# Attention and gated feed-forward on one core: a second queue for the first loads, sign words on a choice of engine, two scales from a sum

## The chip, the core and the metric

The kernel runs on one NeuronCore of a Trainium2 chip. The core has a matrix engine (TensorE, PE in the profile), a vector engine (VectorE, DVE), a scalar engine (ScalarE, ACT), a general engine (GpSimd, POOL) and an engine that issues most transfers (SyncE, SP). Each engine works through its own list of instructions in order, and semaphores tie the lists together. The metric is the device time of one execution in microseconds, lower is better.

## What is computed

Causal attention over 4 batches of 12 heads with 448 tokens of 64 values, then a two-layer feed-forward with a sigmoid gate over the 1792 tokens (768 to 2048 to 768 values):

```python
scores = scale * np.matmul(q, k.transpose(0, 1, 3, 2))
scores = np.where(np.triu(np.ones((seq, seq), dtype=bool), k=1), -1000000000.0, scores)
attn = np.exp(scores - np.max(scores, axis=-1, keepdims=True))
attn = attn / (np.sum(attn, axis=-1, keepdims=True) + 1e-09)
attn_out = np.matmul(attn, v)
x = attn_out.transpose(0, 2, 1, 3).reshape(B * S, H * D)
h = x @ w_in
g = h * (1.0 / (1.0 + np.exp(-1.702 * h)))
out = g @ w_out
```

q, k and v are float32. The weights are float64 and arrive as pairs of 32-bit words.

## The kernel before

**Precision.** Most matmuls take numbers as two float16 parts (a rounded part and the rest), so that a product is three float16 matmuls. The scale that puts the numbers into float16's range is a power of two, found from sums of squares or from the diagonal of a product with itself. `gram` (L609) makes this product on TensorE, `gram_max` (L625) takes the largest value of each row on VectorE, `all_max` (L414) spreads the values of all partitions over a row by a matmul with an identity (`one16`) and takes the largest again, and `norm_scale` (L433) makes the power of two with integer operations on one column. This is done for each slice of w_in ("wi"), for w_out ("wo"), for v, and for each pair of units of k ("k", from a sum of squares on ScalarE).

**Weights.** `to_f32` (L551) makes float32 out of the word pairs in four passes: a scale-down by ScalarE or VectorE (L555), the low words (L563, either engine), the sign words (L586, VectorE) and a combining pass on VectorE (L597). `w_in_slice` (L632) does this for 8 slices of 256 columns. A slice is loaded in two halves of 768 KB into a part of `wob`, all on SP. The slices 0 to 2 (`TUNE["early"]`) are converted in halves of 768 columns, the other ones in one go of 1536. Then `split` (L479) writes the two float16 parts into `wib`. `w_out_load` and `w_out_split` do the same for 16 pieces of w_out; these are parked in unused parts of `wob` and `vraw`.

**Attention.** A batch has 6 units of two heads, and the tokens of a batch form two blocks of 4 and 3 chunks of 64. In batch 0 all units work in float32: `k_unit32` (L900) and `q_unit32` (L917) load heads, turn them on TensorE against `ident` (L885, into `ps_t`, a part of `ps_o`) and copy them into `kT` and `qT`. `q_unit32` writes the two heads of a unit into separate quarters of a `qT` that POOL has filled with zeros, so that one contraction over 128 rows gives one head in each half of the columns (`scores32`, L1081, by `halves`, L409). `chunk` (L1105) adds the mask and finds the row maximum on VectorE (L1112) and exponentiates on ScalarE (L1126); the probabilities are divided, turned on TensorE (L883) into `PT`, and multiplied by v (L1268). From batch 1 on the same is done in float16 parts with transposing transfers.

**Feed-forward.** Each block's tokens go through `h_slice` (L1327): 72 matmuls into a bank of `ps_h`, a tanh on ScalarE (L1362), the gate multiply on VectorE (L1367), and the split into `gT`. The first block alternates between two banks. `out_tile` (L1380) multiplies by w_out (L1405).

**Order.** The kernel's functions don't issue instructions; they add operations with estimated costs to a list (`Ops.add`). `Ops.order` (L103) makes the list of each engine by a search over priorities with random tries that start from `SEED`, and for operations that two engines can do it picks the engine too. So a changed cost or a changed operation can move instructions everywhere.

## Time and profile before

| | us |
|---|---|
| median of 3 runs | 605.53 |
| lowest and highest | 603.63, 605.74 |
| the profiled execution | 605.29 |
| its span, first to last instruction | 603.54 |
| TensorE busy | 575.1 |
| VectorE busy | 416.6 |
| ScalarE busy | 351.6 |
| GpSimd busy | 59.2 |

The page gives the busy time of each engine, its course in 40 slices of about 15 us, the chain of work that ended last, and the costliest groups of instructions. A group names a line, an engine, an operation, what it writes and reads, how often, the busy time, the mean of one instruction, and the idle time of the engine before it. The trace behind the page can be asked for stretches of time (windows), for instructions in order of time, and for groups that keep shapes apart. Matmuls overlap, so that the mean of one is longer than its share of the busy time; float32 matmuls stand as two records each.

### The profile page before, as it was taken

What the parts mean: (1) busy time and instruction counts of PE and PEld (TensorE: products, weight loads), DVE (VectorE), ACT (ScalarE), POOL (GpSimd) and SP (SyncE); (2) the same over time, 40 slices, a digit from 0 to 9 for tenths busy, and PEclk for the clock granted to TensorE, in tenths of its full rate; (3) what the DMA queues carried; (4) which work ended last, traced back from release to release, by engine and by line L of the source; (5) the groups of instructions that cost most, each with busy time, mean ns of one, the idle gap of its engine ahead of it and who ended that gap; (6) DMA issues with size and microseconds to landing.
All of it is one profiled execution on the core that took longest, in us unless ns stands there. A gap on an engine that the chain in (4) does not pass through costs nothing.

```text
span 603.5 us, 22259 instructions
## 1 busy us (share of the span) xinstructions
PE 575.1 (95%) x9526; PEld 501.7 (83%) x9526; DVE 416.6 (69%) x1164; ACT 351.6 (58%) x835; POOL 59.2 (10%) x162
## 2 busy tenths in 40 slices
PE   3876999999999999999999999999999999999997
PEld 2555867886699799977888899998999999889986
DVE  2999999999996889977489887978777122203100
ACT  4888899887866767754676465666355122203110
POOL 3000000012120121212111210211100000000000
PEclk9989899999999999999999999999999999999999
DMA  8998478554498987899997899575835400000000
GB/s 270 277 288 281 128 251 302 173 127 110 86 177 156 142 163 112 167 176 153 156 158 115 155 161 174 105 128 120 130 59 68 94 2 15 1 28 3 28 28 27
DMA packets 201604, 79.90 MB, mean 132 GB/s; under 512 B 182304, under 2 KB 191264, under 8 KB 201504
## 3 DMA queue, kind: packets, MB, share of 16 engines
q1 hardware_dynamic: 201504, 78.47, 61.5%
q8 instruction: 74, 1.21, 0.9%
q14 instruction: 26, 0.21, 0.1%
HBM read 41.68 MB, written 5.51 MB: 78 GB/s over the span
## 4 chain that ended last, share of the span: by engine, by line
PE 68%; DVE 4%; ACT 2%; DMA 1%; issue 1%; SPq 0%; DVEq 0%; ACTq 0%
PE ps_o L1405 33%; PE ps_h L412 26%; PE ps_s L1089 4%; PE ps_v L1268 4%; DVE z L1112 1%; DMA vraw<-in_v_dram 1%; ACT p L472 1%; PE ps_s L412 1%; DVE p L477 1%; PE ps_h L883 1%; DVE ps_h L1367 0%; ACT waste L462 0%; DMA kf<-in_k_dram 0%; DVE q L477 0%; DVE gT L477 0%
## 5 line engine op out<-in xcount | busy, mean ns | idle before, releaser
L412 PE MATMUL ps_h<-xT,wib 128*64 128x256 f16 (+1 forms) x4608 | 244.4, 260 | 0.1
L1405 PE MATMUL ps_o<-wob,gT 128*64 128x384 f16 x2688 | 239.8, 326 | 0.8 <-DVE wob L477 0.6
L412 PEld LDWEIGHTS <-wib 128*64 128x64 f16 x4608 | 226.3, 110 | 7.9 <-issue 2.1
L1405 PEld LDWEIGHTS <-gT 128*64 128x64 f16 x2688 | 171.8, 110 | 38.3 <-issue 3.2
L1126 ACT ACTIVATE z<-z,cols 128x320 f32<-128x320 f32 (+6 forms) x168 | 84.1, 501 | 51.6 <-DVE cols L1112 49.1
L1367 DVE SCALAR_TENSOR_TENSOR ps_h<-t,ps_h 128x512 f32<-128x512 f32 (+1 forms) x64 | 40.1, 626 | 82.4 <-ACT t L1362 82.0
L1362 ACT ACTIVATE t<-ps_h,cols 128x512 f32<-128x512 f32 (+1 forms) x64 | 40.3, 629 | 72.1 <-PE ps_h L412 68.0
L1112 DVE CUSTOM_DVE_ANT_0 z<-ps_s,mask,cols 128x128 f32<-128x128 f32 (+6 forms) x126 | 57.2, 479 | 18.0 <-PE ps_s L1089 17.4
L477 DVE SCALAR_TENSOR_TENSOR p<-z,cols,p 128x128 f16<-128x128 f32 (+3 forms) x126 | 63.2, 528 | 1.5 <-ACT p L472 0.8
L477 DVE SCALAR_TENSOR_TENSOR gT<-ps_h,gT 128x512 f16<-128x512 f32 (+1 forms) x64 | 39.7, 620 | 13.5 <-ACT gT L472 13.1
L1268 PE MATMUL ps_v<-PT,v 128*64 128x192 f16 (+7 forms) x792 | 44.7, 257 | 0.5 <-DVE cols L453 0.4
L1089 PE MATMUL ps_s<-kT,qT 128*64 128x64 f16 (+4 forms) x504 | 41.5, 273 | 1.2 <-DVE cols L1112 0.9
L472 ACT ACTIVATE p<-z,cols 128x384 f16<-128x384 f32 (+3 forms) x66 | 34.0, 533 | 13.3 <-DVE cols L1235 9.7
L472 ACT ACTIVATE gT<-ps_h 128x512 f16<-128x512 f32 (+1 forms) x53 | 28.9, 545 | 20.4 <-DVE ps_h L1367 20.3
L472 ACT ACTIVATE ob<-ps_o,cols 128x384 f32<-128x384 f32 x24 | 13.8, 577 | 45.0 <-PE ps_o L1405 44.6
L1126 ACT ACTIVATION_READ_ACCUMULATOR z<-z,cols 128x1 f32 x168 | 31.6, 188 | 0.0
L412 PE MATMUL ps_s<-kT,qT 128*64 128x320 f32 (+6 forms) x168 | 25.0, 409 | 5.6 <-DVE cols L1112 5.6
L1268 PEld LDWEIGHTS <-v 128*64 128x64 f16 x648 | 29.2, 110 | 1.0
L1089 PEld LDWEIGHTS <-qT 128*64 128x64 f16 x504 | 24.7, 110 | 4.3 <-issue 1.3
L1047 POOL TENSOR_SCALAR q<-q 128x512 f16<-128x512 f16 (+1 forms) x32 | 21.9, 686 | 50.8 <-ACT q L472 26.6
L474 DVE TENSOR_SCALAR p<-z,cols 128x256 f16<-128x256 f32 (+3 forms) x60 | 24.6, 422 | 1.3
L472 ACT ACTIVATE wob<-wob 128x768 f32<-128x768 f32 (+1 forms) x20 | 21.8, 1091 | 5.5 <-DMA wob<-in_moe_w_in_dram 5.0
(98 smaller groups left out, 564.9 us busy)
## 6 DMA issues: line engine op xcount, KB each, us to landing
wob<-in_moe_w_in_dram SPq DMA_DIRECT2D x16, 768.0 KB, 6.5
wob<-in_moe_w_out_dram SPq DMA_DIRECT2D x9, 768.0 KB, 6.2
vraw<-in_moe_w_out_dram SPq DMA_DIRECT2D x7, 768.0 KB, 6.7
out_dram<-ob SPq DMA_DIRECT2D x28, 192.0 KB, 2.2
kf<-in_k_dram SPq DMA_DIRECT2D x36, 112.0 KB, 3.3
vraw<-in_v_dram SPq DMA_DIRECT2D x9, 384.0 KB, 5.0
qf<-in_q_dram SPq DMA_DIRECT2D x48, 64.0 KB, 3.1
qf<-in_q_dram SPq DMA_DIRECT2D x48, 48.0 KB, 3.2
```

What stands on the lines that cost most here:

```text
L412: nc.tensor.matmul(out[o : o + 64], lhsT[:, o : o + 64], rhs, start=start, stop=stop)
L472: nc.scalar.activation(out=dst, in_=src, func=AF.Copy, scale=sc)
L474: nc.vector.tensor_scalar(out=dst, in0=src, scalar1=sc, scalar2=None, op0=ALU.mult)
L477: nc.vector.scalar_tensor_tensor(out=dst, in0=src, scalar=sc, in1=hi, op0=ALU.mult, op1=ALU.subtract)
L1047: nc.gpsimd.tensor_scalar(out=dst, in0=src, scalar1=1.0, scalar2=1.0, op0=ALU.mult, op1=ALU.mult)
L1089: nc.tensor.matmul(ps[64 * j : 64 * j + 64], qt[:, g, i - c0, 64 * j : 64 * j + 64], kt[:, : i + 1, 64 * j : 64 * j + 64], start=(g == 0), ...
L1112: lambda e: nc.vector.tensor_tensor_reduce(out=z[:, :w], in0=ps, in1=mask[:, S - w :], scale=c, scalar=3.0e38, op0=ALU.add, op1=ALU.min, a ...
L1126: lambda e: nc.scalar.activation(out=z[:, :w], in_=z[:, :w], func=AF.Exp, bias=m, scale=-1.0, accum_out=l),
L1268: nc.tensor.matmul(ps[64 * j : 64 * j + 64, 64 * (first - c0) : w], vt[:, J, j] if f32(b, u) else vt[:, gv, J, j, :], (p_f32(pi)[:, at] if ...
L1362: lambda e: nc.scalar.activation(out=th, in_=ph, func=AF.Tanh, scale=ts[:, sl : sl + 1]),
L1367: lambda e: nc.vector.scalar_tensor_tensor(out=ph, in0=th, scalar=1.0, in1=ph, op0=ALU.add, op1=ALU.mult),
L1405: nc.tensor.matmul(po[64 * j : 64 * j + 64, :OH], gT[:, f, gg, 64 * r : 64 * r + 64], wo_pair(f, gw, nh), start=(f == 0 and gg + gw == 0), ...
```

## The change

It does these things:

- The four loads of the slices 0 and 1 of w_in (`beside=2`) are issued by ScalarE, on its own queue ("AQ" in the planner), ahead of everything else on that engine. All other loads stay on SP.
- All 8 slices are converted in halves (`early=8`).
- The sign words can be made by ScalarE as well: a copy to float16 of numbers that have been scaled down to almost nothing leaves only the sign.
- For k and w_out, `all_max` puts a matmul with a column of ones (`total`) in place of the spread and of the maximum; the sum over the partitions, one column, is read by `norm_scale` from PSUM.
- `q_unit32` copies both heads of a unit at once and needs no zeros; `scores32` contracts over 64 rows for each head.
- The planner knows the second queue, has a lower cost for issuing a load, and starts from another seed, so all lists are ordered anew.

```diff
@@ TUNE, Ops
-    early=3,
+    early=8,
+    beside=2,
-SEED = 2
+SEED = 1
-    ENGINES = ("SP", "PE", "ACT", "DVE", "POOL")
+    ENGINES = ("SP", "AQ", "PE", "ACT", "DVE", "POOL")
-    LOAD = 0.68
+    LOAD = 0.5
+    BESIDE = 1.4
...
@@ kernel
+    ones16 = cols[:, 174:175].bitcast(BF16)[:, 0:1].to_broadcast([P, 64])
+    def total(out, src):
+        for o in range(0, P, 64):
+            nc.tensor.matmul(out[o : o + 64], ones16, src, start=True, stop=True)
...
@@ all_max
+        if tag in ("k", "wo"):
+            half = src.bitcast(BF16)[:, 1:2]
+            add(
+                {"PE": 0.03},
+                lambda e: total(row[:, :1], half),
+                [src_key, "one16"], row_keys, prio,
+            )
+            return row[:, :1], row_keys[0]
...
@@ to_f32
+        def sign(e):
+            if e == "ACT":
+                nc.scalar.activation(
+                    out=words(dst, F16, 2)[..., 1], in_=words(raw, F32, 2)[..., 1], func=AF.Copy
+                )
+            else:
...
         add(
-            dve(n, rate=0.521),
...
+            {**dve(n, rate=0.521), **act(n, rate=1.0)},
+            sign,
             raw_keys, dst_keys, prio,
         )
@@ w_in_slice
-                {"SP": Ops.LOAD},
-                lambda e, h=h: nc.sync.dma_start(
+                {"AQ" if s < TUNE["beside"] else "SP": Ops.LOAD},
+                lambda e, h=h: (nc.scalar if e == "AQ" else nc.sync).dma_start(
@@ q_unit32
-        if stale[t]:
...
-        for j in range(2):
...
+        add(
+            {**act(64 * ni, psum=True, rate=1.2), **dve(64 * ni, rate=1.2)},
+            lambda e: scaled(e, qt.rearrange("p (x t) -> p x t", t=2), got, 1.0),
+            [got_key], [key], prio,
+        )
+        return qt, key, -QK_SCALE, None
@@ scores32
-                halves(ps, qt[:, i - c0].rearrange("p j w -> p (j w)"), kt[:, : 64 * (i + 1)], True, True)
+                for j in range(2):
+                    x = slice(64 * j, 64 * j + 64)
+                    nc.tensor.matmul(
+                        ps[x], qt[x, 64 * (i - c0) : 64 * (i - c0) + 64], kt[x, : 64 * (i + 1)], start=True, stop=True
+                    )
@@ the end
-        for i, e in ops.order():
+        for i, e in sorted(ops.order(), key=lambda x: x[1] != "AQ"):
```

SP's list, which issues the loads, at its start, before. `q_76` and `qf` are the buffers of the first k and q heads, `wob` takes the weight halves, `v_70` to `v_72` the first v:

```order
L875 DMA q_76<-in_k_dram 128x128 x2
L648 DMA wob<-in_moe_w_in_dram 128x3x512
L875 DMA qf<-in_q_dram 128x128 x2
L648 DMA wob<-in_moe_w_in_dram 128x3x512
L817 DMA v_71<-in_v_dram 128x4x64
L875 DMA q_76<-in_k_dram 128x128
```

The same place after:

```order
L909 DMA qf<-in_q_dram 128x128
L909 DMA q_76<-in_k_dram 128x128
L909 DMA qf<-in_q_dram 128x128
L909 DMA q_76<-in_k_dram 128x128
L909 DMA qf<-in_q_dram 128x128 x2
L909 DMA q_76<-in_k_dram 128x128 x2
```

The weight halves have left the start of SP's list; its first one is now the 17th row, behind 22 loads of q, k and v.

ScalarE's list at its start, before. `ACT_TABLE_LOAD` and the row behind it fetch the table for exp, `wob` rows convert weights, `qT` and `kT` rows copy turned heads:

```order
L531 ACT_TABLE_LOAD
L531 ACTIVATE cols<-cols 128x1
L472 ACTIVATE wob<-wob 128x768
L566 ACTIVATE wob<-wob 128x768
L472 ACTIVATE qT_77<-ps_o_97 64x4x64
L472 ACTIVATE wob<-wob 128x768
```

The same place after:

```order
L683 DMA wob<-in_moe_w_in_dram 128x3x512 x4
L557 ACT_TABLE_LOAD
L557 ACTIVATE cols<-cols 128x1
L497 ACTIVATE qT_77<-ps_o_97 128x256
L497 ACTIVATE wob<-wob 128x768
L497 ACTIVATE qT_78<-ps_o_97 128x256
L615 ACTIVATE wob<-wob 128x768
```

The four weight loads stand ahead of the table load, the copy of the first q stands ahead of the first weight pass, and a sign pass (L615) has come in.

VectorE's list at its start, before. `z` rows (ISA) are score chunks, L588 makes sign words, L599 combines, L574 makes low words:

```order
L474 TENSOR_SCALAR qT_77<-ps_o_97 64x4x64
L588 TENSOR_SCALAR wob<-wob 128x768
L599 SCALAR_TENSOR_TENSOR wob<-wob 128x768
L588 TENSOR_SCALAR wob<-wob 128x768
L599 SCALAR_TENSOR_TENSOR wob<-wob 128x768
L1112 ISA z,cols<-ps_s_91,mask 128x64
```

The same place after, where L600 makes low words and L1136 is the score chunk:

```order
L499 TENSOR_SCALAR kT_67<-ps_o_97 128x256
L600 TENSOR_SCALAR wob<-wob 128x768
L1136 ISA z,cols<-ps_s_91,mask 128x128
L1136 ISA cols 128x1
L1136 ISA z,cols<-ps_s_91,mask 128x64
```

The first score chunk stands behind one weight pass, where four stood ahead of it.

## Rows read from the trace of the kernel before

**Rows 1.** The page: busy time of each engine; TensorE in 40 equal slices, in tenths.

```profile
PE 575.1 (95%) x9526; PEld 501.7 (83%) x9526; DVE 416.6 (69%) x1164; ACT 351.6 (58%) x835; POOL 59.2 (10%) x162
...
PE   3876999999999999999999999999999999999997
```

**Rows 2.** Windows: stretch, its length, busy us (instructions) by engine, clock, DMA, GB/s.

```profile
0.00:14.55 14.55, 4.85 (x36) 3.59 (x38) 3.53 (x6) 6.72 (x10) 4.54 (x22) 1.00 0.84 269
14.55:70.00 55.45, 44.04 (x616) 32.40 (x614) 53.16 (x169) 46.03 (x112) 0.00 (x0) 0.94 0.92 268
70.00:123.44 53.44, 51.49 (x836) 43.04 (x834) 52.59 (x117) 50.91 (x94) 0.81 (x1) 1.00 0.64 215
123.44:172.98 49.54, 48.88 (x698) 36.45 (x694) 46.66 (x129) 39.30 (x89) 8.02 (x17) 1.00 0.57 108
172.98:595.00 422.02, 420.76 (x7303) 382.21 (x7299) 260.66 (x746) 207.47 (x532) 45.82 (x122) 1.00 0.59 104
```

**Rows 3.** Timeline, 0 to 15 us: start, us, engine, line, what, count, [idle before].

```profile
0.80 0.87 SPq L875 DMA_DIRECT2D q<-in_k_dram  x2
...
1.72 0.43 SPq L648 DMA_DIRECT2D wob<-in_moe_w_in_dram  x1
...
2.19 0.96 SPq L875 DMA_DIRECT2D qf<-in_q_dram  x2
...
6.76 0.89 ACT L472 ACTIVATE wob<-wob 128x768 f32<-128x768 f32 x1 [4.47 <-DMA wob<-in_moe_w_in_dram]
...
7.26 1.12 PE L893 MATMUL ps_o<-ident,qf 128*64 128x128 f32 x8 [7.26 <-DMA qf<-in_q_dram]
...
11.04 1.11 PE L893 MATMUL ps_o<-ident,q 128*64 128x128 f32 x6 [1.05 <-DMA q<-in_k_dram]
...
14.55 0.23 DVE L1112 CUSTOM_DVE_ANT_0 z<-ps_s,mask 128x64 f32<-128x64 f32 x1 [1.96 <-PE ps_s L412]
```

**Rows 4.** DMA issues, q loads: the whole program (page), then 0 to 30 us.

```profile
qf<-in_q_dram SPq DMA_DIRECT2D x48, 64.0 KB, 3.1
...
qf<-in_q_dram SPq DMA_DIRECT2D x12, 64.0 KB, 5.2
```

**Rows 5.** Groups by form on VectorE: line, what, shapes, count | busy us, mean ns | idle.

```profile
L599 DVE SCALAR_TENSOR_TENSOR wob<-wob 128x768 int32<-128x768 int32 x15 | 14.1, 948 | 0.4 <-ACT wob L566 0.3
...
L588 DVE TENSOR_SCALAR wob<-wob 128x768 uint16<-128x768 uint16 x15 | 9.0, 607 | 0.3 <-ACT wob L472 0.3
L599 DVE SCALAR_TENSOR_TENSOR wob<-wob 128x1536 int32<-128x1536 int32 x5 | 8.7, 1747 | 0.0
...
L588 DVE TENSOR_SCALAR wob<-wob 128x1536 uint16<-128x1536 uint16 x5 | 5.2, 1045 | 0.0
...
L628 DVE TENSOR_REDUCE cols<-ps_s 128x1 f32<-128x128 f32 x12 | 3.5, 288 | 4.2 <-PE ps_s L412 4.2
...
L474 DVE TENSOR_SCALAR z<-z,cols 128x256 f32<-128x256 f32 x8 | 2.6, 346 | 0.1
...
L474 DVE TENSOR_SCALAR qT<-ps_o 64x256 f32<-64x256 f32 x4 | 1.6, 412 | 7.7 <-PE ps_o L893 7.5 <-ACT kT L472 0.2
```

**Rows 6.** Groups by form on ScalarE: scale-down of a half, low words.

```profile
L472 ACT ACTIVATE wob<-wob 128x768 f32<-128x768 f32 x15 | 13.7, 914 | 5.5 <-DMA wob<-in_moe_w_in_dram 5.0 <-DMA wob<-in_moe_w_out_dram 0.5
...
L566 ACT ACTIVATE wob<-vraw 128x768 uint16<-128x768 uint16 x4 | 4.3, 1083 | 1.1 <-DVE wob L599 1.1
```

**Rows 7.** Timeline of VectorE: the ninth gate multiply.

```profile
172.98 0.56 DVE L1367 SCALAR_TENSOR_TENSOR ps_h<-t,ps_h 128x384 f32<-128x384 f32 x1 [0.37 <-ACT t L1362]
```

**Rows 8.** Groups by form on TensorE, 0 to 160 us: scores of batch 0's last chunks; maxima of k.

```profile
L412 PE MATMUL ps_s<-kT,qT 128*64 128x448 f32 x24 | 5.7, 549 | 1.1 <-DVE cols L1112 1.1
...
L412 PE MATMUL ps_s<-kT,qT 128*64 128x384 f32 x24 | 5.0, 494 | 0.0
...
L412 PE MATMUL ps_s<-kT,qT 128*64 128x320 f32 x24 | 4.3, 437 | 0.8 <-DVE cols L1112 0.8
...
L412 PE MATMUL ps_s<-one,cols 128*64 128x128 bf16 x6 | 0.7, 227 | 0.1
```

60 lines of the change are left out of this document (26 added, 34 removed).

## The prediction

> **What bounds the kernel now.** I read four views, in this order: the page's totals and slices, the windows of each engine, the timeline of the first 15 us, and the groups by form. TensorE is busy for 575.1 of the span [rows 1], so most of the program is a full TensorE, and from 172.98 us to 595 us it is idle for 422.02 - 420.76 = 1.26 us only [rows 2]. Nothing in the change touches that stretch except some short matmuls. The slices show where time can be had: TensorE's digits are 3, 8, 7, 6 before the nines begin [rows 1]. By the windows it stands idle for 14.55 - 4.85 = 9.7 us up to 14.55 us, for 11.4 us from there to 70 us and for 2.6 us from 70 to 172.98 us [rows 2]. In the same stretches VectorE has something to do for 53.16 of 55.45, 52.59 of 53.44 and 46.66 of 49.54 us, whereas before 14.55 us it works for 3.53 us. So the start has two limits. Up to 14.55 us everything waits for loads, and from there VectorE sets the pace, with ScalarE close behind it (50.91 of 53.44 us from 70 to 123 us). As a mark for the end of this stage I take the ninth gate multiply on VectorE (L1367, the first of block 1), which stands at 172.98 us [rows 7]. Behind it TensorE is the bound, and ahead of it the two orders hold nearly the same matmuls. What the mark gains, the end gains.
>
> The sum is made against the profiled execution, 605.29 us: its span of 603.54 and 1.75 around it. The median of the runs shown is 0.24 us above it.
>
> **Part 1, the first loads.** Before, two k loads, the first weight half (768 KB) and the first two q loads stand in one queue in this order. The q loads are issued from 2.19 us and the turn that needs them starts at 7.26; the second half of k lets the next turns run at 11.04, and VectorE has its first score chunk at 14.55 [rows 3]. After, SP issues q, k, q, k first, and the four weight halves leave through ScalarE's queue. Two issues took 0.87 and 0.96 us, so the fourth is out at 0.80 + 0.87 + 0.96 = 2.63 us. A 64 KB q load lands after 3.1 us as a median of the program, and after 5.2 us in the crowded first 30 us [rows 4], so the four are there at 5.7 to 7.8 us, against 11.04. That is 3.2 to 5.3 us earlier for the first chunk. No row has two queues at once, so the lower end of what this gives is nothing, if the 3 MB of weights press the small loads back to where they were. I take 4.0 us, from near the middle of what the rows give. ScalarE pays four issues at 0.43 us [rows 3] ahead of its table load; the 4.47 us that it waits for the first weights there cover these 1.7 us.
>
> The first half of the weights is issued at 1.72 us now and is scaled at 6.76 us. After, it leaves about 0.9 us earlier and shares the wires with 256 KB of q and k; I put that at no change.
>
> The Trainium skill (DMA: Bandwidth & Descriptors, section "Issuing engines are not separate DMA queues") says that DMAs of all issuing engines run on the same 16 engines and interleave, so that a second issuer saves only issue time. Of this rule alone, part 1 would be worth the 1.7 us of four issues, and the sum below would end near 602.8. The row speaks for more, since the q loads stood behind a 768 KB load in their own queue and not only behind its issue.
>
> **Part 2, VectorE's list up to the mark.** Counted in the orders, piece by piece, at the durations of [rows 5]:
> - The slices 3 to 7 are converted in halves: 5 combining passes of 1.747 us become 10 of 0.948, +0.7 us.
> - The passes for low words and signs: ten of 1536 columns at 1.045 us go, seventeen of 768 columns at 0.607 us come, -0.1 us. Six sign passes that ScalarE takes are in this.
> - Seven q copies of at most 0.412 us go, which I count as -2.7 us (four of 256 columns, three of 192), since one copy of 128 partitions does what two of 64 did, and ScalarE does all of them. Three k copies of the same width come, +1.2 us.
> - Five reductions at 0.288 us go (three of k, two of w_out), -1.4 us.
> - The rest differs by which engine was chosen. Seven 256-wide passes on z at 0.346 us leave (-2.4), three of 128 and two of 512 columns come (by width +1.8), and all other differences are about as many added as removed; I put them at +0.5, with 1 us either way.
>
> Together -2.4 us. VectorE is busy for 155.9 us up to the mark, so its idle time there is 17.0 us, 11.0 of it before 14.55 us [rows 2]. If nothing else limits, the mark moves by 4.0 + 2.4 = 6.4 us.
>
> **Part 3, ScalarE's list.** Up to its ninth tanh it gets six sign passes, priced at the 0.914 us of the scale-down of the same size (+5.5); it loses three low-word passes at 1.083 us (-3.2) [rows 6]; the four issues come (+1.7), and what moved over from VectorE, less the merged q copies, is +2.0. Together +6.0 us, and at the first tanh it is already +7.5. Up to the mark ScalarE is busy for 143.0 of 172.98 us. The 30 us of slack cover this as a whole, but from 70 to 123.44 us there are only 2.5 us of slack [rows 2], and until then the list is longer by 6 to 8 us. What stands queued behind it there is tanh, then the gate multiply on VectorE, then the release of the two ps_h banks of block 0. So some of the gain is lost to ScalarE; I take off 1.9 of the 6.4 us (bounds 0 and 6.4, the latter as a rival below). That leaves 4.5 us.
>
> **Part 4, TensorE.** The maxima of k over the partitions were pairs of 128 columns, six records in 0.7 us up to 160 us [rows 8], eighteen more behind; a pair of one column takes their place. That is 12 pairs of some 0.1 us, of which I count 0.5 us (bounds 0 and 1.2). The memsets of qT on POOL go; no one waits for POOL there. The scores of batch 0 contract over 64 rows now, one head in the upper and one in the lower half of the rows, where a zero-padded q had used all 128. Number and width of the matmuls stay, so I put it at nothing, as long as the two matmuls of a pair run beside each other as they do before. No row shows a matmul on the lower 64 rows alone. Bounds: 15.0 us more in the rival below, and nothing saved, since the columns are the same.
>
> Sum: 4.5 + 0.5 = 5.0 us, 605.29 - 5.0 = 600.3 in the profiled execution's terms, and **600.5 us** as a median. Its own range is 597 to 602.4: the first loads between 3.2 and 5.3, the loss to ScalarE between 0 and 3.
>
> **Rivals.**
> *ScalarE becomes the bound of the start* (604.2). For it: it gets 6 to 8 us more work ahead of a stretch in which it was 95% busy, and the first tanh stands seven microseconds deeper in its list. Against it: 7.8 us of idle time before 14.55 us and 9.4 us from there to 70 us. If all of the 4.5 us goes, the 0.5 of TensorE and something of the earlier start, 0.8, remain of the gain.
>
> *The two queues do not help* (605). The weights, in flight four at a time, take what the small loads had won; the chunk at 14.55 stays, VectorE's 2.4 are lost to ScalarE. That is the case in which the change does not do what it says.
>
> *The pairs of scores run one after the other* (615.5, slower). The groups of 448, 384 and 320 columns take 5.7 + 5.0 + 4.3 = 15.0 us now [rows 8], all in block 1's share, most of it behind 70 us where TensorE is 97% busy. If the two row halves exclude each other, each pair takes up to twice its time, and 15.0 us come on top of 600.3. It decides from 8 us on, that is when over half of the overlap in these pairs is lost; the narrower groups of block 0 fall into TensorE's idle time. Against it: in before the two halves of the columns do run beside each other, and the new pair uses separate rows and columns.
> The Trainium skill (TensorEngine Tiling (Array Packing), section "Restrictions and Gotchas") states that different row tiles cannot access the same PSUM bank simultaneously, and both halves of such a pair write one bank. By that rule this rival would hold; no run so far shows it.
>
> *All of it carries* (595): VectorE's 6.4 us in full, the earlier first loads at their upper end, 1.3 more, and 1.2 + 1.3 from TensorE and from its idle time behind the mark.
>
> **How the numbers follow.** Forecast 0.48, ScalarE 0.22, queues 0.10, pairs 0.12, all of it 0.08. Half a per cent, 3 us, is about what a measurement of this kernel can tell from no change. Faster by over that (below 602.5): 0.48 + 0.08 and 0.02 of the ScalarE case, 0.58. Within: 0.20 + 0.10, less 0.02 that the queues take to the slow side, 0.28. Slower: 0.12 + 0.02 = 0.14. The range from 594.5 to 608.5 leaves out the pairs and little else.
>
> **What would show it.** First turn on TensorE at 5 to 6 us, first score chunk on VectorE before 11 us; the ninth gate multiply at 167 to 170 us; VectorE busy about 153.5 us up to there; score groups of 448 columns still 5 to 6 us in total. Wrong if the first chunk is still at 14 us, if ScalarE shows no idle time from 15 to 120 us while VectorE waits for it, if the score groups take twice their time, or if the gaps of TensorE behind the mark grow beyond 1.3 us.

## The result, and the profile after

The changed kernel took 607.72 us in the median of 7 runs (605.22 to 611.83), the kernel before 604.51 beside it (603.63 to 606.42): 1.0054 times the time, 95% interval 1.0033 to 1.0076. It is slower by half a per cent, where 600.5 us was forecast. The profiled execution took 607.27 us, span 605.6, against 605.29 and 603.54.

The page of the changed kernel: busy time of each engine, TensorE in 40 slices, and its granted clock in the same slices.

```profile
PE 578.4 (96%) x9526; PEld 503.3 (83%) x9526; DVE 408.2 (67%) x1151; ACT 356.3 (59%) x847; POOL 57.3 (9%) x157
...
PE   4887889999999999999999999999999999999997
...
PEclk9989899999999999999999999999999999999999
```

VectorE has 8.4 us less to do than in [rows 1] and ScalarE 4.7 us more, as the change meant. But TensorE, which runs the same number of matmuls, is busy for 3.3 us longer, 578.4 against 575.1. Its idle time, span less busy, went from 28.4 to 27.2 us. So the kernel lost 3.3 us of TensorE's busy time and won back 1.2 us of waiting. The forecast had 0.5 us of busy time and 4.5 us of waiting to win.

Windows of the changed kernel, with a cut at its own ninth gate multiply (stretch, length, busy us of PE, PEld, DVE, ACT, POOL, clock, DMA, GB/s), and the two gate multiplies, first and ninth:

```profile
0.00:14.55 14.55, 5.98 (x42) 3.96 (x44) 1.58 (x8) 4.71 (x11) 3.34 (x19) 1.00 0.87 277
14.55:174.39 159.84, 148.83 (x2184) 109.23 (x2182) 151.23 (x415) 141.94 (x305) 10.17 (x21) 0.98 0.75 201
174.39:595.00 420.61, 416.54 (x7224) 384.33 (x7220) 255.40 (x731) 208.53 (x531) 43.76 (x117) 1.00 0.60 103
...
80.15 0.68 DVE L1391 SCALAR_TENSOR_TENSOR ps_h<-t,ps_h 128x512 f32<-128x512 f32 x1
...
174.39 0.56 DVE L1391 SCALAR_TENSOR_TENSOR ps_h<-t,ps_h 128x384 f32<-128x384 f32 x1
```

The mark, 172.98 us in [rows 7], moved to 174.39, later by 1.4 us and not earlier by 4.5. Up to it TensorE waits for 14.55 - 5.98 + 159.84 - 148.83 = 19.6 us, against 23.7 us in [rows 2]: the waits there did shrink by 4.1 us, close to what was forecast for them, and 40 more matmul records lie ahead of the mark (42 + 2184 = 2226, against 36 + 616 + 836 + 698 = 2186 in [rows 2]), so that the mark does not stand behind quite the same work in the two orders. Behind the mark TensorE waits for 420.61 - 416.54 = 4.1 us, against 1.26 us before. 2.8 us are given back there. These are the longest of the waits, from the view of who waited for whom, TensorE from 173 us on (who, for whom: us in total, times, longest):

```profile
PE ps_h L425 <- DVE gT L502: 1.2, 1, 1.2
PE ps_s L1113 <- DMA qT<-q: 1.1, 1, 1.1
PE ps_s L1113 <- DMA kT<-k: 0.9, 1, 0.9
```

Two of the three are transposing transfers of the next batch that are not there in time. The start answers to [rows 3] like this (timeline of the changed kernel):

```profile
0.79 7.93 ACTq L683 DMA_DIRECT2D wob<-in_moe_w_in_dram  x4
...
7.72 1.11 PE L927 MATMUL ps_o<-ident,qf 128*64 128x128 f32 x6 [3.92 <-DMA qf<-in_q_dram]
...
8.59 1.12 PE L927 MATMUL ps_o<-ident,q 128*64 128x128 f32 x8
...
8.75 1.28 ACT L557 ACT_TABLE_LOAD   x1 [8.75 <-DMA wob<-in_moe_w_in_dram]
...
10.16 0.37 ACT L497 ACTIVATE qT<-ps_o 128x256 f32<-128x256 f32 x1
10.42 0.90 ACT L497 ACTIVATE wob<-wob 128x768 f32<-128x768 f32 x1
...
11.85 0.42 DVE L499 TENSOR_SCALAR kT<-ps_o 128x256 f32<-128x256 f32 x1 [10.92 <-PE ps_o L927]
...
13.40 0.29 DVE L1136 CUSTOM_DVE_ANT_0 z<-ps_s,mask 128x128 f32<-128x128 f32 x1 [0.61 <-PE ps_s L1105]
```

ScalarE is held for 7.93 us by its four issues; its table load starts at 8.75, its first copy at 10.16, the first weights are scaled at 10.42 (6.76 before), and VectorE has its first score chunk at 13.40 (14.55 before). That chunk needs the copy of the first k, which starts at 11.85 us only, although k was turned by 8.59 + 1.12 = 9.71 us. The section on the first loads comes back to this. The runs below take the row halves (the scores of batch 0 over 64 rows for each head), the first loads, the sign words and the sums one at a time. The conversion of all slices in halves, and with it the new order as a whole, was not undone by itself.

### The profile page after: what moved, and what is told of

The parts are those of the page before. It is cut to its first block, busy times and chain, and to the rows that moved or that the text cites. A ratio compares the mean times of both kernels' runs of the same rounds, so it can differ in the third digit from the quotient of the medians.

```text
span 605.6 us, 22243 instructions
## 1 busy us (share of the span) xinstructions
PE 578.4 (96%) x9526; PEld 503.3 (83%) x9526; DVE 408.2 (67%) x1151; ACT 356.3 (59%) x847; POOL 57.3 (9%) x157
## 4 chain that ended last, share of the span: by engine, by line
PE 73%; DVE 9%; DMA 9%; ACT 4%; issue 2%; SPq 2%; ACTq 0%; POOL 0%; DVEq 0%
PE ps_o L1429 30%; PE ps_h L425 29%; PE ps_v L1292 4%; PE ps_s L1113 3%; PE ps_s L1105 3%; DMA qf<-in_q_dram 3%; DMA kT<-k 2%; DVE z L1136 2%; DMA kf<-in_k_dram 2%; PE ps_o L425 1%; PE ps_h L917 1%; DMA wob<-in_moe_w_in_dram 1%; ACT z L1150 1%; DMA q<-in_k_dram 1%; DVE wib L502 1%
## 5 line engine op out<-in xcount | busy, mean ns | idle before, releaser
L1429 PEld LDWEIGHTS <-gT 128*64 128x64 f16 x2688 | 175.5, 110 | 35.1 <-issue 3.4
L1136 DVE CUSTOM_DVE_ANT_0 z<-ps_s,mask,cols 128x448 f32<-128x448 f32 (+6 forms) x126 | 57.3, 479 | 17.3 <-PE ps_s L1113 16.6
L502 DVE SCALAR_TENSOR_TENSOR p<-z,cols,p 128x256 f16<-128x256 f32 (+3 forms) x126 | 62.0, 524 | 4.2 <-ACT p L497 3.2
L1292 PE MATMUL ps_v<-PT,v 128*64 128x192 f16 (+7 forms) x792 | 43.4, 251 | 1.3 <-DVE xT L502 0.7
L497 ACT ACTIVATE p<-z,cols 128x128 f16<-128x128 f32 (+3 forms) x70 | 35.9, 534 | 13.2 <-DVE cols L1259 8.7
L1105 PE MATMUL ps_s<-kT,qT 64*64 64x320 f32 (+6 forms) x168 | 27.5, 437 | 5.8 <-DVE cols L1136 2.7
L1068 POOL TENSOR_SCALAR q<-q 128x384 f16<-128x384 f16 (+1 forms) x31 | 22.7, 735 | 36.3 <-ACT q L497 22.4
L1253 POOL TENSOR_SCALAR cols<-cols 128x2 f32<-128x2 f32 (+1 forms) x48 | 11.8, 246 | 151.7 <-ACT z L1150 149.6
L499 DVE TENSOR_SCALAR p<-z,cols 128x384 f16<-128x384 f32 (+3 forms) x56 | 23.3, 430 | 1.3 <-DVE cols L1259 0.3
```

The lines of the kernel that those rows point to most:

```text
L497: nc.scalar.activation(out=dst, in_=src, func=AF.Copy, scale=sc)
L499: nc.vector.tensor_scalar(out=dst, in0=src, scalar1=sc, scalar2=None, op0=ALU.mult)
L502: nc.vector.scalar_tensor_tensor(out=dst, in0=src, scalar=sc, in1=hi, op0=ALU.mult, op1=ALU.subtract)
L1105: nc.tensor.matmul(ps[x], qt[x, 64 * (i - c0) : 64 * (i - c0) + 64], kt[x, : 64 * (i + 1)], start=True, stop=True)
L1136: lambda e: nc.vector.tensor_tensor_reduce(out=z[:, :w], in0=ps, in1=mask[:, S - w :], scale=c, scalar=3.0e38, op0=ALU.add, op1=ALU.min, a ...
L1292: nc.tensor.matmul(ps[64 * j : 64 * j + 64, 64 * (first - c0) : w], vt[:, J, j] if f32(b, u) else vt[:, gv, J, j, :], (p_f32(pi)[:, at] if ...
```

## The experiments

Most experiments keep the order of their kernel, frozen instruction by instruction, and change one thing in it. Times are medians; ratios are to the kernel before on the same chip, with 95% intervals. The kernel before has medians between 604.02 and 605.18 us there, so two kernels are compared by their ratios and not by their times. Costs are given in points, hundredths of the time of the kernel before (one point is 6 us). a_rows128 and a_rows128_signs compute other numbers: a score is there the sum over both heads of a unit.

| kernel | base | what is different | us | ratio |
|---|---|---|---|---|
| changed | | | 607.72 | 1.0054 (1.0033 to 1.0076) |
| b_rows64 | before | row halves | 607.4 | 1.0049 (1.0025 to 1.0073) |
| b_rows64_n0 | before | row halves, block 0 | 605.59 | 1.0027 (1.0013 to 1.0042) |
| b_rows64_n1 | before | row halves, block 1 | 607.0 | 1.0041 (1.0027 to 1.0056) |
| b_merge | before | row halves, one q copy | 606.73 | 1.0023 (1.0007 to 1.0039) |
| a_rows128 | changed | 128 rows, one q copy, heads summed | 603.8 | 0.9995 (0.9978 to 1.0012) |
| a_pad | changed | 128 rows, two q copies | 607.46 | 1.0027 (1.0012 to 1.0042) |
| b_actq | before | ScalarE issues four loads | 608.6 | 1.0066 (1.0048 to 1.0084) |
| a_two_two | changed | ScalarE issues two, later two | 609.21 | 1.0069 (1.0043 to 1.0095) |
| a_spq | changed | SP issues all | 606.54 | 1.0032 (1.0015 to 1.0048) |
| a_loads | changed | SP issues all, order of before | 606.43 | 1.0017 (0.9997 to 1.0037) |
| a_signs | changed | signs on VectorE | 604.67 | 1.0007 (0.9991 to 1.0023) |
| a_rows128_signs | changed | a_rows128 and a_signs | 605.67 | 1.0004 (0.9988 to 1.0021) |
| b_total | before | sums for k and w_out | 606.8 | 1.0019 (1.0005 to 1.0033) |
| a_pad_signs | changed | a_pad and a_signs | 607.79 | 1.0040 (1.0020 to 1.0061) |
| a_pad_signs_spq | changed | the same and a_spq | 608.29 | 1.0065 (1.0040 to 1.0089) |
| a_signs_loads | changed | a_signs and a_loads | 606.36 | 1.0033 (1.0015 to 1.0051) |

### The row halves

First theory: the second queue or ScalarE cost the time. First rival: the scores in row halves, for which the prediction had put nothing. The kernel before, with that alone (b_rows64):

```diff
-                halves(ps, qt[:, i - c0].rearrange("p j w -> p (j w)"), kt[:, : 64 * (i + 1)], True, True)
+                for j in range(2):
+                    x = slice(64 * j, 64 * j + 64)
+                    nc.tensor.matmul(ps[x], qt[x, i - c0, j], kt[x, : 64 * (i + 1)], start=True, stop=True)
```

> The kernel before, where only the matmuls of batch 0's scores change: each head contracts over its own 64 rows, as in the changed kernel, and the zeros are no longer read. The order of every engine is that of before. If the pairs lose part of their overlap, the f32 score groups, 25.0 us in before and 27.5 in the changed kernel, come to about 27.5 us here and the time rises by 0.5 to 2.5 us (605 to 607). If the 2.5 us in the changed kernel come from other things (clock, neighbours in the order), the groups stay at 25 us and the time at that of before, within 1 us.

It took 607.4 us, 1.0049, just above the first of the two ranges. This one edit costs as much as the whole change. Its score groups by form from 14.55 us to the old mark (busy us, mean ns), beside [rows 8]:

```profile
L1085 PE MATMUL ps_s<-kT,qT 64*64 64x448 f32 x24 | 5.8, 562 | 1.2 <-DVE cols L1114 1.1
...
L1085 PE MATMUL ps_s<-kT,qT 64*64 64x384 f32 x24 | 5.2, 508 | 0.0
L1085 PE MATMUL ps_s<-kT,qT 64*64 64x320 f32 x24 | 4.5, 455 | 0.7 <-DVE cols L1114 0.7
```

The pairs do run beside each other: 24 records of 562 ns are 13.5 us and take 5.8, against 5.7 for the same columns over 128 rows. So the rival with its price of 15 us is out. The three groups grew by 0.5 us in all, which doesn't explain 2.9. The next three kernels ask where the rest is: the edit in block 0 alone, in block 1 alone, and the reverse edit in the changed kernel. For block 1 (block 0 with `n != 0`), and for the changed kernel:

```diff
+                if n != 1:
+                    halves(ps, qt[:, i - c0].rearrange("p j w -> p (j w)"), kt[:, : 64 * (i + 1)], True, True)
+                    continue
```

```diff
-                        ps[x], qt[x, 64 * (i - c0) : 64 * (i - c0) + 64], kt[x, : 64 * (i + 1)], start=True, stop=True
+                        ps[x], qt[:, 64 * (i - c0) : 64 * (i - c0) + 64], kt[:, : 64 * (i + 1)], start=True, stop=True
```

> The kernel before, in which only block 0 of batch 0 (groups of 64 to 256 columns, most of them before 75 us) has its scores in row halves. Theory A1, the row halves cost in the start stage, where TensorE's granted clock is not at its upper level throughout: 606.5 to 607.5, nearly all of the 2.5 us that both blocks cost together. Theory A2, they cost by their columns: the groups of block 1 hold 15 of 26.5 us, so here 605.8 to 606.2.

> The kernel before, in which only block 1 of batch 0 (groups of 320 to 448 columns) has its scores in row halves. Each of its 18 groups was 0.03 to 0.04 us longer with them, 0.6 us in sum. Theory A1 (the cost lies in the start stage): 605.0 to 605.8. Theory A2 (the cost goes with the columns): 606.2 to 606.8.

> The changed kernel, in which only the scores of batch 0 contract over all 128 rows again (the same instructions, columns and order; the two heads are summed, so these scores are other numbers than the reference's). Theory A, the row halves cost about 3 us wherever they stand, as they did alone in the kernel before: 604 to 605.5 us, 2 to 3.5 us below the changed kernel. Theory B, what the row halves cost in the kernel before was its own order and not the form: 607 to 608, as the changed kernel. In the trace the groups of 448 columns are 0.91 to 0.94 us long in place of 0.97.

Block 0 alone cost 1.6 us, block 1 alone 2.5. The theory that nearly all of the cost lies in the start stage was wrong: block 1 alone is slower by 0.27 to 0.56 points. Which block has the larger part is within the noise. In the changed kernel 128 rows took 0.59 points off, 3.6 us (1.0054 to 0.9995), and its page shows TensorE at 574.9 us instead of 578.4, with the same list in the same order:

```profile
PE 574.9 (96%) x9526; PEld 504.9 (84%) x9526; DVE 407.8 (68%) x1151; ACT 356.5 (59%) x847; POOL 57.5 (10%) x157
```

Where block 1 loses is seen in the order of time. TensorE in the kernel before, and then the same place in b_rows64_n1 (start, us, line, what, count of records):

```profile
142.70 1.47 PE L1405 MATMUL ps_o<-wob,gT 128*64 128x384 f16 x16
144.00 0.70 PE L412 MATMUL ps_s<-kT,qT 128*64 128x320 f32 x4
144.54 2.12 PE L1405 MATMUL ps_o<-wob,gT 128*64 128x384 f16 x24
146.49 0.94 PE L412 MATMUL ps_s<-kT,qT 128*64 128x448 f32 x4
```

```profile
143.41 2.12 PE L1410 MATMUL ps_o<-wob,gT 128*64 128x384 f16 x24
145.45 0.76 PE L1088 MATMUL ps_s<-kT,qT 64*64 64x320 f32 x4
146.14 1.17 PE L1410 MATMUL ps_o<-wob,gT 128*64 128x384 f16 x12
```

Read the starts, not the durations. Before, 24 matmuls take 146.49 - 144.54 = 1.95 us from the first one's start to the next group, 0.163 per pair, as for the 16 ahead of the first group (144.00 - 142.70 = 1.30): the group starts while their last pair still runs. The score group holds TensorE for 0.54 us (144.00 to 144.54). With row halves the same 24 matmuls last 145.45 - 143.41 = 2.04 us until the group may start, 0.09 more, and the group holds TensorE for 0.69 us, 0.15 more. So this group costs 0.24 us, though its own duration grew by 0.06 only. Where the form changes from 128 rows to 64 rows and back, the matmuls on either side don't overlap as they did. The loss adds up over the groups; the first and the ninth gate multiply of b_rows64_n1 stand 0.1 us and 1.9 us behind those of the kernel before (76.82 us and, in [rows 7], 172.98):

```profile
76.93 0.68 DVE L1372 SCALAR_TENSOR_TENSOR ps_h<-t,ps_h 128x512 f32<-128x512 f32 x1
...
174.91 0.56 DVE L1372 SCALAR_TENSOR_TENSOR ps_h<-t,ps_h 128x384 f32<-128x384 f32 x1 [0.20 <-ACT t L1367]
```

18 groups of 0.24 us would be 4.3 us, more than the 2.5 that block 1 cost; some have a neighbour of yet another form (the turns of z, 128*128), and some fall into waits.

To measure the change of form by itself, 56 pairs of one column were added to the kernel before, in one kernel over 64 rows, in the other over 128 (there with `one16[:, o : o + 64], one16[:, :1]`):

```diff
                 def mm(e, a=a, t=t):
+                    if n and t and not a:
+                        for o in range(0, P, 64):
+                            nc.tensor.matmul(ph[o : o + 64, 1, :1], one16[o : o + 64, o : o + 64], one16[o : o + 64, :1], start=True, stop=True)
                     for u in range(a, a + half):
```

> The kernel before with 56 added pairs of matmuls of one column each (64 x 1 into a place that the next matmul overwrites), one ahead of a run of 128-row matmuls in each gate slice of blocks 1 to 7, in row halves: rows 0 to 63 into the upper, rows 64 to 127 into the lower half. Theory S, a change between the 128-row and the 64-row form costs TensorE 0.1 us on either side since the next matmul doesn't start beside the last one: 56 x 0.2 to 0.25 = 11 to 14 us more than the same pairs over 128 rows. Theory A, only the columns count: no difference between the two.

> The kernel before with the same 56 added pairs of one column each, over all 128 rows, the form of their neighbours. The pairs of one column that sum over the partitions in the changed kernel are of this form. By both theories 56 x 0.03 to 0.06 us = 2 to 3.5 us over the kernel before, most of it behind 173 us, where TensorE is the bound.

One run each: 615.4 and 606.07 us, against 604.61 for the kernel before. The difference is 9.3 us, 0.17 us for each pair, a little under what was expected; the pages have it as TensorE's busy time, 586.2 against 576.9. The timeline of b_tiny64, then of b_tiny128, for the same piece of the list:

```profile
561.93 0.19 PE L1341 MATMUL ps_h<-one 64*64 64x1 bf16 x2
562.05 0.93 PE L412 MATMUL ps_h<-xT,wib 128*64 128x192 f16 x18
562.91 0.19 PE L1341 MATMUL ps_h<-one 64*64 64x1 bf16 x2
```

```profile
553.54 0.17 PE L1341 MATMUL ps_h<-one 128*64 128x1 bf16 x1
...
554.31 0.17 PE L1341 MATMUL ps_h<-one 128*64 128x1 bf16 x1
```

From one added pair to the next it is 0.98 us with 64 rows and 0.77 with 128, for the same 18 matmuls and two small ones. A pair of one column over 128 rows costs some (606.07 - 604.61) / 56 = 0.03 us; that is an estimate from one run, and the 1.5 us lie within the spread of the kernel before (602.27 to 606.66). The 9.3 us between the two don't: the price sits in the change of form.

The change takes a copy of q away for what it pays here. Is the trade a loss? In the kernel before, with one copy and row halves (b_merge, the first diff beside the one of b_rows64), and in the changed kernel with two copies and 128 rows (a_pad, the second, with `halves` for the scores and the zeros written once by POOL ahead of everything):

```diff
-                lambda e, j=j: scaled(
-                    e,
-                    qt[64 * j : 64 * j + 64, :ni, j].rearrange("p c (x t) -> p c x t", t=2),
...
+                lambda e, j=j: j or scaled(e, qt.rearrange("p (x t) -> p x t", t=2), got, 1.0),
```

```diff
-            lambda e: scaled(e, qt.rearrange("p (x t) -> p x t", t=2), got, 1.0),
+            lambda e: [
+                scaled(
+                    e,
+                    qt[64 * j : 64 * j + 64, :ni, j].rearrange("p c (x t) -> p c x t", t=2),
...
+                for j in range(2)
+            ],
```

> The kernel before with the q part of the change alone, at the same places of the order: one copy of q over 128 partitions where there were two of 64 (11 fewer, 8 on ScalarE and 3 on VectorE), and the scores of batch 0 in row halves. The row halves alone made it 607.4 (1.0049 of the kernel before, 2.9 us). If the copies saved pay for the changes of form: 604.5 to 605.5. If they save what a second copy cost in the changed kernel's order, 0.003 of the time or 1.9 us: 605.5 to 606.2. If copies on ScalarE save nothing here: 607 to 608.

> The changed kernel with q in its zero-padded form (two copies of 64 partitions each, 128-row contraction), signs left on ScalarE. Against the kernel with 128 rows and one copy (603.8) it prices the second copies: if they cost what their durations say, 12 x 0.3 to 0.4 us and half of it hidden, 605.5 to 607; if they cost all that the row halves saved or more, 607.5 to 610.

b_merge: 1.0023, between 1.0049 with two copies and 1. a_pad: 1.0027, between 1.0054 and 0.9995. By the medians the saved copies are worth 0.26 to 0.32 points in both orders (some 1.7 us), the changes of form cost 0.49 to 0.59 (3 to 3.6 us), and the trade loses 0.23 and 0.27. The cost of the forms is clear of the intervals; the 0.26 for the copies is not, and the 0.27 for the trade only just. With the sign passes on VectorE neither holds: 64 rows stand at 1.0007 (a_signs), 128 rows with one copy at 1.0004 (a_rows128_signs), 128 rows with two copies at 1.0040 (a_pad_signs). TensorE is busy for 1.4 us longer with 64 rows there too (577.0 against 575.6 us), but that falls into waits. So what the row halves cost in the end depends on the order around them. The windows of the kernel before and then of b_merge show both sides of the trade; PE's counts are the matmul records done:

```profile
14.55:64.00 49.45, 38.04 (x518) 27.33 (x516) 47.16 (x150) 40.78 (x104) 0.00 (x0) 0.94 0.96 288
64.00:173.00 109.00, 106.38 (x1626) 84.58 (x1624) 105.26 (x264) 95.48 (x189) 8.82 (x18) 1.00 0.61 160
```

```profile
14.55:64.00 49.45, 40.69 (x569) 28.02 (x566) 47.00 (x152) 40.24 (x102) 0.00 (x0) 0.97 1.00 295
64.00:173.00 109.00, 106.81 (x1579) 80.61 (x1575) 104.00 (x258) 93.42 (x184) 9.47 (x18) 1.00 0.61 157
```

At 64 us b_merge is 51 records ahead (part of it by the clock, 0.97 against 0.94). From there to 173 us it is busy longer and does 47 fewer. In this pair of traces, what the copies win where VectorE and ScalarE set the pace, the forms lose where TensorE does.

### The first loads

```diff
-                lambda e, h=h: nc.sync.dma_start(
+                lambda e, h=h: (nc.scalar if s < 2 else nc.sync).dma_start(
...
```

> The kernel before, where only the four loads of the slices 0 and 1 move to ScalarE's queue, ahead of all else there; every other order stays. By the prediction's part 1 the first score chunk comes 3 to 5 us earlier than 14.55 us and the time falls by 3 to 4 us (601). If issuing four loads in a row holds ScalarE for about 8 us, as the changed kernel's trace has it, the table load ends at about 10 us, the first weight pass starts at 10 instead of 6.76 us, and the time is that of before or up to 3 us more (604 to 608).

b_actq took 608.6 us (1.0066), above both of its expectations. Its ScalarE is held even longer than that of the changed kernel, its first weight pass starts at 10.96 us (6.76 before), and its first q is turned at 8.92 us (7.26 before), with the weights in flight beside its load:

```profile
0.80 8.73 ACTq L651 DMA_DIRECT2D wob<-in_moe_w_in_dram  x4
```

The next two kernels take the hold away in the changed kernel, once by leaving two of the four issues for later (behind ScalarE's 2nd and 4th instruction), once by giving all four to SP behind its 4th, 8th, 12th and 16th load:

```diff
+        for i in aq[:2]:
+            ops.ops[i][1]("AQ")
...
+            if e == "ACT":
+                seen += 1
+                if seen in (2, 4):
+                    ops.ops[aq[1 + seen // 2]][1]("AQ")
```

```diff
+            if e == "SP":
+                seen += 1
+                if seen in (4, 8, 12, 16):
+                    ops.ops[aq[seen // 4 - 1]][1]("SP")
```

> The changed kernel, where ScalarE issues only the two loads of slice 0 ahead of everything and the two of slice 1 behind its first q copy and behind its second. All other orders stay. If the hold of 7.93 us at the first four issues is what took the gain, ScalarE is held for about 1 us, its table load ends before 3.5 us, the first score chunk comes at about 9 us instead of 13.40, and the time falls by 3 to 4 us against the changed kernel (604). If ScalarE's longer list or the order behind is what costs, the start moves but the time stays within 1 us of the changed kernel (607 to 608).

> The changed kernel without the second queue: the four loads go back to SP's list, behind its 4th, 8th, 12th and 16th load of q, k and v; all other orders stay. If the hold of ScalarE is the cost, this frees ScalarE as well, q and k still go first, and the time is 603 to 606. If the second queue itself helps, the weights come later here and the time is that of the changed kernel or more (607 to 611).

a_two_two missed what was expected of it (609.21 us): two issues hold ScalarE for 1.01 us only, but its first copy still starts at 9.91 us, since it waits for TensorE: the second head of q is turned from 7.81 us on, when its load is there, and k behind it until 9.86. The first chunk is at 13.19 us, 0.2 us earlier than in the changed kernel. So the hold is not what set the start there.

```profile
0.80 1.01 ACTq L683 DMA_DIRECT2D wob<-in_moe_w_in_dram  x2
...
9.91 0.38 ACT L497 ACTIVATE qT<-ps_o 128x256 f32<-128x256 f32 x1 [6.58 <-PE ps_o L927]
```

In a_spq the second head of q is turned from 3.97 us on, that copy stands at 5.97 us and the first chunk at 11.73, 2.8 us earlier than before. With the weights behind the small loads in one queue the start comes near what the prediction wanted:

```profile
3.97 0.90 PE L927 MATMUL ps_o<-ident,qf 128*64 128x128 f32 x5 [0.55 <-DMA qf<-in_q_dram]
...
5.97 0.38 ACT L497 ACTIVATE qT<-ps_o 128x256 f32<-128x256 f32 x1 [3.69 <-PE ps_o L927]
...
10.19 0.42 DVE L499 TENSOR_SCALAR kT<-ps_o 128x256 f32<-128x256 f32 x1 [9.26 <-PE ps_o L927]
...
11.73 0.29 DVE L1136 CUSTOM_DVE_ANT_0 z<-ps_s,mask 128x128 f32<-128x128 f32 x1 [0.61 <-PE ps_s L1105]
...
175.50 0.56 DVE L1391 SCALAR_TENSOR_TENSOR ps_h<-t,ps_h 128x384 f32<-128x384 f32 x1
```

What is left of the wait is no load of the first unit: k was turned by 5.93 us, and its copy starts at 10.19. In the traces of the changed kernel, a_two_two, a_spq and a_loads it starts 0.13 to 0.16 us behind the end of the next turn on TensorE, that of the second unit's q, which waits for its own load or for the copy of the first q. In the kernel before, the first copy of q starts 0.04 us behind its own turn (7.26 + 1.12 = 8.38 us, then 8.42). The prediction had no term for this, and no run undoes it.

And yet the ninth gate multiply of a_spq is at 175.50 us, behind the 174.39 of the changed kernel, and the time is 1.0032, between its two expectations. In that trace the granted clock was 0.78 from 14.55 to 30 us and 0.71 from 30 to 40, against 1.00 and 0.83 in the changed kernel, so the clock is one candidate for what became of the lead; no run tests it. To see whether the order of the loads matters at all, a_loads puts them as in the kernel before (k, k, weights, q, q, weights) on SP:

```diff
+        for i in (sp[1], sp[3], aq[0], sp[0], sp[2], aq[1]):
+            ops.ops[i][1]("SP")
...
```

> The changed kernel with its first loads in the order of the kernel before and on SP alone: k, k, first weight half, q, q, second half; the other two halves behind SP's 8th and 12th load. If the early loads of q and the second queue are worth something: 608.5 to 611, since VectorE's first chunk comes 1 us and more later. If the start is decided elsewhere: 606 to 608, as with SP alone (1.0032) and two queues (1.0054).

606.43 us, 1.0017 (0.9997 to 1.0037): not slower than any of the other variants of the loads. Its first chunk is at 12.85 us, earlier than the 13.40 of the changed kernel, so even that did not need the second queue. Neither the second queue nor the early q gave anything that reaches the end. That the loads on ScalarE's queue cost is shown in the order of the kernel before (b_actq), where the hold and the late small loads come together; in the changed order the kernel without the hold was no faster (a_two_two, 1.0069).

### The sign words and the sums

```diff
         def sign(e):
-            if e == "ACT":
+            if False:
```

> The changed kernel with its six sign passes that ScalarE made put back on VectorE, at the same places of the order. If ScalarE is what holds the start back: 604.5 to 606 us, since ScalarE's list is shorter by 5.5 us and VectorE's longer by 3.6 to 5.7. If VectorE is the one that is short of time there: 609 to 611. If neither: 607 to 608.

604.67 us, 1.0007. Taken alone this says that the signs on ScalarE cost 2.8 us. The traces don't bear out that ScalarE was the reason. Up to 67 us the two kernels stand within 0.1 us of each other. Then TensorE's timeline, first of the changed kernel, then of a_signs:

```profile
66.83 0.55 PE L917 MATMUL ps_h<-ident,z 128*128 128x128 f32 x3 [1.27 <-ACT PT L497]
67.70 0.83 PE L927 MATMUL ps_o<-ident,q 96*64 96x96 f32 x8 [0.33 <-DMA q<-in_k_dram]
68.46 1.75 PE L1105 MATMUL ps_s<-kT,qT 64*64 64x448 f32 x4
70.15 3.65 PE L425 MATMUL ps_h<-xT,wib 128*64 128x256 f16 x54
```

```profile
66.92 0.55 PE L917 MATMUL ps_h<-ident,z 128*128 128x128 f32 x3 [1.29 <-ACT PT L497]
67.39 0.55 PE L927 MATMUL ps_o<-ident,q 96*64 96x96 f32 x8
67.88 0.97 PE L1105 MATMUL ps_s<-kT,qT 64*64 64x448 f32 x4
68.78 3.14 PE L425 MATMUL ps_h<-xT,wib 128*64 128x256 f16 x54
```

The same group of 448 columns takes 1.75 us in one and 0.97 in the other. The windows say why (changed kernel, then a_signs; the number behind POOL's is the granted clock):

```profile
65.00:70.00 5.00, 3.40 (x20) 1.42 (x19) 4.99 (x14) 4.84 (x10) 0.00 (x0) 0.78 0.30 70
```

```profile
65.00:70.00 5.00, 3.71 (x42) 2.42 (x44) 5.00 (x14) 5.00 (x10) 0.00 (x0) 1.00 0.33 73
```

In the changed kernel the clock is at its lower level (1.2 of 2.4 GHz) for part of this stretch, in which TensorE had stood idle for 1.6 us; in a_signs it is not, though TensorE stood idle for 1.3 us there too. VectorE then waits for TensorE (2.0 us in one piece, 0.8 in a_signs), and at 80.15 us the first gate multiply is 1.9 us behind that of a_signs. So in this pair of traces most of the difference up to there goes with the clock, and some 0.3 us with the wait for a load of q at 67.70. Whether that reaches the end is another matter: a_rows128 had a clock of 0.87 and 0.79 from 65 to 70 and from 70 to 75 us and its first gate multiply at 80.80 us, and it took 0.9995. The other test is the same edit where the row halves are gone:

> The changed kernel with the scores of batch 0 contracted over 128 rows (the two heads summed, so other numbers than the reference's, and no second copy of q) and the six sign passes back on VectorE. If the two parts add up and what kept the padded kernel at 607.8 were its second copies: 600.5 to 602. If the two parts make room in the same place: 603 to 604.5. If the moved signs are only good with the row halves: 605 to 607.

605.67 us, 1.0004, against 0.9995 without the edit. Here the signs on ScalarE cost nothing. What a_signs gained stays open between ScalarE's list and the clock; that ScalarE is the bound is not shown. In the order of the changed kernel the row halves and the signs on ScalarE cost 3.6 and 2.8 us only where both are present: either one undone brings the time of the kernel before, and undoing both brings no more. Why is open.

The sums were tried alone in the kernel before:

```diff
-            lambda e: halves(row, top, one16, True, True),
+            lambda e: total(row[:, :1], src.bitcast(BF16)[:, 1:2])
+            if tag in ("k", "wo")
+            else halves(row, top, one16, True, True),
...
```

> The kernel before with only the sum over the partitions for the scales of k and w_out: a pair of one column in place of a pair of 128 columns and a reduction, its first step reads the sum at the place where the reduction stood, the order otherwise the same. By the sum of the prediction 0.5 us from TensorE and up to 1.4 from VectorE's five reductions ahead of 173 us: 602.5 to 604. If only what lies behind 173 us counts: 603.9 to 604.5.

606.8 us, 1.0019 (1.0005 to 1.0033). Less work in the same order, and no gain; if anything a small loss, which stays unexplained.

### Putting parts together

These three join edits that are shown above: two copies of q with 128 rows and the signs on VectorE; the same with all loads on SP; the signs on VectorE with the first loads of a_loads.

> The changed kernel with two of its parts undone at the same places of the order: the six sign passes of ScalarE are on VectorE, and q goes into its zero-padded form again, in two copies of 64 partitions, so that the scores of batch 0 contract over 128 rows. Undone one by one these gave 3.6 us (0.9995 against 1.0054) and 2.8 us (1.0007). If they add up, less about 1 us for the twelve additional copies: 601.5 to 603, faster than the kernel before by 0.2 to 0.5 %. If both only make room in the same stretch, and one of them is enough: 603.5 to 604.5.

> As the kernel of this set with both parts undone, and the four early weight loads issued by SP behind its 4th, 8th, 12th and 16th load, so that there is one queue and ScalarE starts free. If what the one queue gave the changed kernel (1.0032 in place of 1.0054, 1.2 us) adds up as well: 600.5 to 602. If the queue makes no difference once ScalarE has its signs off: the time of its neighbour, within 0.7 us.

> The changed kernel with the sign passes back on VectorE and its first loads in the order of the kernel before and on SP alone; row halves and merged copies kept. Undone alone these gave 1.0007 and 1.0017 of the kernel before. If they add up with the 1.0054 of the changed kernel (-0.0047 and -0.0037): 0.997, 602.5 to 603.8, and it beats both kernels. If the parts make room in the same place, as signs and row halves did: 604.5 to 605.8.

1.0040, 1.0065 and 1.0033: by its median each is slower than every one of its parts alone, where the gains in sum would have brought it to 0.996 to 0.998. Some of these steps are within the noise (1.0033 against the 1.0017 of a_loads), but that the gains don't add is not: the lower ends are 1.0015 to 1.0040. Why they don't is open. No kernel here beats both; a_rows128, a_signs and a_rows128_signs come to the time of the kernel before.

## Why the prediction was wrong, point by point

**TensorE (part 4) is the step that failed.** The row halves were put at nothing "as long as the two matmuls of a pair run beside each other". They do run beside each other, and yet the edit costs 2.9 us in the kernel before and 3.6 in the changed one, through the overlap with the matmuls on either side of a pair that is lost where the form changes (0.24 us in the group shown, 0.17 us for each added pair of b_tiny64). This explains the loss against the kernel before, and with it half of the miss of 7.2 us: with 128 rows (a_rows128) the time is that of the kernel before and the mark stands at 173.44 us, still not ahead of 172.98, so the 5 us of the forecast are missing there as well. The points below are about those; what became of them is known in part only. The prediction asked only whether the halves of a pair exclude each other and not what stands on either side of it. Its rival had the right place and side, with another mechanism and 15 us. The Trainium skill's rule on this (TensorEngine Tiling (Array Packing), "Restrictions and Gotchas"), that row tiles cannot access one PSUM bank at the same time, is not borne out here: the two matmuls of a 448-column group write one bank, one from rows 0 to 63 into partitions 0 to 63, the other from rows 64 to 127 into partitions 64 to 127, and the group takes 0.97 us, against 0.94 over 128 rows. The 0.5 us for the sums were not seen either (b_total).

**The first loads (part 1)** were put at 4.0 us; the first chunk came 1.15 us earlier. Two terms were wrong and one was missing. The four issues were taken at 0.43 us each, 1.7 in all; they held ScalarE for 7.93 us, and its table load and the first q copy are queued behind them (though a_two_two, without the hold, had its first chunk only 0.2 us earlier). And the q loads, said to land at 5.7 to 7.8 us, let the turn of the second head start at 7.72 us, the late end of that range and no earlier than the 7.26 for both heads before, although they were issued first. Nor was the start before all a matter of loads: from the first turn at 7.26 us to the first chunk at 14.55, TensorE waits for a load for 1.05 us only [rows 3]. The missing term is the copy of k, which starts 2.1 us behind the end of its turn and only after that of the next q. The Trainium skill (DMA: Bandwidth & Descriptors, "Issuing engines are not separate DMA queues") says that DMAs of all engines interleave; the rows agree, since the small loads came early only where SP had them ahead of the weights (a_spq, 3.97 us in place of 7.72). The deeper miss is the carry: even the 2.8 us of a_spq's first chunk were not there at its mark.

**VectorE (part 2)** went as counted: 152.8 us up to the mark, where 153.5 were said. The step from there, that the mark moves with VectorE's list, did not hold: VectorE stood idle for 21.6 us up to the mark instead of 17.0.

**ScalarE (part 3)**: +3.7 us up to the mark (146.7 against 143.0) instead of +6.0. Of the 6.0, 1.7 were the four issues, which busy time doesn't count; without them it is 4.3 against 3.7. As a rival it is neither shown nor excluded: with six passes less on ScalarE the changed kernel gained 2.8 us (a_signs), the one with 128 rows nothing (a_rows128_signs).

**The mark.** It came 1.4 us later instead of 4.5 earlier, and "What the mark gains, the end gains" was wrong in itself. TensorE's waits ahead of the mark shrank by 4.1 us, near the forecast 4.5; as the mark also lies behind 40 more records, that agreement may be chance. But behind it they grew from 1.26 to 4.1 us, which the prediction named as a sign of being wrong and gave no price. In a_rows128, the same order with 128 rows, they are 1.5 us behind its own mark (the row below); in a_pad, with 128 rows and two copies, 3.4 us from 172.98 us on. Which transfers come late there differs from kernel to kernel, and what decides it was not settled.

```profile
173.44:595.00 421.56, 420.02 (x7276) 386.25 (x7273) 255.12 (x731) 208.46 (x531) 44.09 (x117) 1.00 0.60 103
```

Chances: "same" and "slower" had 0.42 between them; the result, 1.0054 with an interval from 1.0033, lies on the border of the two. That 607.72 us lies inside the wide range is luck: none of the rivals gives this time by the mechanism that the runs show.

## What to carry to other kernels

Before a matmul changes how many rows or columns of the array it uses, look at its neighbours in TensorE's list: here each switch to a 64-row pair and back cost TensorE 0.17 to 0.24 us where the neighbours had overlapped, in two of three kernels this reached the end, and a copy saved on another engine didn't pay for it. Before an engine that computes issues several large loads in a row, ask how long they hold it and what is queued behind them. A gain read at a mark inside the kernel must be followed to the end, through the waits that come later.

## What the runs showed of the hardware that was not expected

- A row half beside a full contraction: the start of the next matmul moves by 0.09 us ahead of the group and 0.15 us in and behind it, while the durations of the records hardly change. The group's own busy time and mean hide it; the starts show it, and so does TensorE's busy time as a whole (578.4 us against 574.9 in a_rows128).
- Four issues of 768 KB on ScalarE's queue held the engine for 7.93 (the changed kernel) and 8.73 us (b_actq), two for 1.01 us (a_two_two).
- The time of the changed kernel and its variants goes with TensorE's granted clock, that of the kernel before doesn't. The correlation of a run's time with its mean clock is -0.79 over the 7 runs of the changed kernel and between -0.34 (a_pad) and -0.84 (a_pad_signs) over 7 to 12 runs of each of its variants, about 0.1 to 0.5 us for a thousandth of the clock; in the five sets of 19 to 35 runs of the kernel before it is between -0.17 and 0.33. The variants of the kernel before are on either side (-0.94 for b_rows64 over 7 runs, -0.03 for b_total over 12). Both kernels have stretches at the lower level, before 75 us. In the kernel before they seem to fall into time in which TensorE waits anyway; that is a reading of two traces, not a test.
